# High halves of first-layer weights at their buffers' release, two decodings a phase, and other buffers for phase 8's turned tiles

## Chip, core and metric

The kernel runs on one core of a Trainium2 chip. The metric is the device time of one execution in microseconds (us). The engines are TensorE (PE), VectorE (DVE), ScalarE (ACT), GpSimd (POOL) and SyncE (SP); SP issues all the DMAs of this kernel.

## What is computed

An attention with decaying state, then a layer of eight experts with normalized weights P, then a last layer with a two-sided activation. Everything is float32. This is the reference, cut to what matters here:

```python
x = attention(q, k, v)                        # 1536 x 512
for e in range(8):                            # moe_w1: 512 x 1024, moe_w2: 1024 x 512 each
    h = np.maximum(x @ w1[e], 0.0)
    out += P[:, e:e + 1] * (h @ w2[e])
h = out @ w_in                                # 512 x 2048
g = np.maximum(h, 0.0) + alpha * np.minimum(h, 0.0)
return g @ w_out                              # 2048 x 512
```

w_in and w_out come as 64-bit floats; the kernel turns them into 32-bit floats itself. That is the decoding below.

## The kernel before

**Phases.** After the attention, 20 phases follow one another. Phases 0 to 7 are the eight experts on the first 768 tokens, 8 to 15 the eight experts on the other 768, 16 and 17 the two halves of the last layer on the first tokens, 18 and 19 the same on the others. Phases 8 to 15 are called fast (`FAST`): they also use seven products instead of eight in the second layer. The others are called slow.

**Split numbers.** Each float32 matrix is split into a high part (ACT copies it to the matmul's reduced format) and a low part (the rest, a subtraction on DVE or POOL). `mm3` (line 195) multiplies high x high, high x low and low x high, so each pair of matrices costs three matmuls.

**Product stage.** Every phase begins with it. The first layer is done with seven products instead of eight (a scheme of sums and differences of quarter matrices), for four column groups j = 0 to 3, n = 4 x phase + j. So there are 28 products (j, p) with p = 1 to 7. Each is six matmuls of 384 columns. The order is written out by hand in `order` (line 902). A place in it is called a position here:

```
0 (0,1)   1 (0,5)   2 (0,6)   3 (0,2)   4 (0,7)   5 (1,1)   6 (1,5)
7 (0,4)   8 (1,6)   9 (0,3)  10 (1,2)  11 (1,7)  12 (2,1)  13 (2,5)
14 (1,4) 15 (2,6)  16 (1,3)  17 (2,2)  18 (2,7)  19 (3,1)  20 (3,5)
21 (2,4) 22 (3,6)  23 (2,3)  24 (3,2)  25 (3,7)  26 (3,3)  27 (3,4)
```

`after` (line 686) is what follows each product. After p = 1, ACT copies bank A to a new bank B (line 698), and p = 6, 7 and 4 add to B. After p = 5, ACT copies bank D to `d` (line 693 in the fast phases and those of experts). After p = 6, DVE makes bank E = B + d (line 701). Product (j,7) may then add to B. After p = 7, DVE makes D = B + d (line 714, slow) or `b22` = B + d (line 709, fast), and (j,4) may then add to B. After p = 2, 3, 4 ACT takes the result out.

**Second half.** In a slow phase it is layer 2: six blocks t of tokens, each in two half-blocks `t0a`, `t0`, ... `t5`, of 12 matmuls of 512 columns each. DVE adds each block's result to `total` (line 749). Positions 28 to 39 are these half-blocks. In a fast phase it is `fast2` (line 829), 28 units of six matmuls of 384 columns, on seven pieces `hs` of the hidden layer that ACT (`hhigh`) and DVE (`t1` to `t4`, `hlow`) make of `b11`, `b12`, `b21`, `b22`. Positions 28 to 55 are these units. Its results, weighted by DVE (line 823), are added to `total` by POOL in the next phase (`gather`, line 825). A position of 60 or more is a position of the next phase (60 is 0).

**What is hung in.** `step(ph, pos, fn)` (line 911) hangs a piece of work behind a position; within one position the pieces come in the order in which they were registered. Every engine runs its own instructions strictly in this order (`tc.manual_schedule`), and waits for the semaphores of the data and the buffers that it needs. The pieces are:
- `w1_at` (line 937): for one n, the sums of first-layer weights (`w1_adds`, not in the fast phases, which read them ready), then high and low halves of the parts a (A11, A12, used by p = 1, 2), c (W1 to W3, used by p = 5, 6, 7) and b (A22, W4, used by p = 4, 3). The tiles `wa`, `wb`, `wc` have two buffers a tag (`wp`), so the tile for n + 2 takes the buffer of n. The low half of part b also asks for the raw tile of n + 2 (`w_load`).
- the second layer's weights: `w2_high`, `w2_low`, `w2_keep` (stored for the fast phases).
- `prep_at` (line 926): for one piece of the second layer's weights, the sums for the fast phases (two and two, on DVE or POOL), the load of the next piece, the high half (ACT), two low halves (DVE) and the store. There are 32 pieces, five a phase in phases 1 to 6, two in phase 7.
- `decode_at` (line 918): one of 32 units of w_in and w_out. `bits` is three DVE operations, `power` one of ACT, `join` two of DVE, `store` a store of 256 KB and the load of the next unit (512 KB, tile `rd`, one buffer). The unit's tiles `ex` and `a` have the tag `tmp`, which has two buffers.
- `turn` (line 884): at the end of phase 7 and the start of phase 8 it turns `total` (three transpositions on PE, a copy on ACT into a tile with the tag `tmp`, a store), eight times.

The order around the change is this part of the loop over phases:

```python
            if fast:
                w1_at(ph, n + 2, pool, dve, 0, 2, 3, 3, 5, 5, 7)
                w1_at(ph, n + 3, pool, dve, 5, 9, 14, 10, 15, 12, 16)
...
                decode_at(ph, *((11, 13, 14, 16) if ph == E else (9, 11, 12, 13)))
                decode_at(ph, *((22, 24, 26, 27) if ph == E else (20, 22, 23, 25)))
                if ph < 2 * E - 1:
                    decode_at(ph, 53, 55, 60, 61)
```

The numbers of `w1_at` are the positions of the sums, then of high and low for a, c and b. Those of `decode_at` are bits, power, join and store.

Of the kernel before, what the change touches and what calls it, by code (L numbers as in the profile page):

```python
# [8 lines left out]
F32 = mybir.dt.float32  # L9
# [35 lines left out]
def tile_kernel(ctx, tc, qkT, kv, ctab, w_gate, w1, w2, w_in, w_out, alpha, out):  # L45
# [246 lines left out]
    with tc.manual_schedule():  # L292
# [591 lines left out]
        def turn(g, a, h):  # L884
            ps = bank(f"tr{g}_{a}{h}")
            for q in range(3):
                nc.tensor.matmul(
                    ps[:, 128 * q:128 * q + 128], acc[3 * h + q][:, 128 * a:128 * a + 128], ident,
                    start=(q == 0), stop=(q == 2), is_transpose=True, skip_group_check=True,
                )  # L890
            t = tp.tile([128, HT], F32, tag="tmp", name=f"tt{g}_{a}{h}")
            nc.scalar.activation(out=t, in_=ps[:, 0:HT], func=AF.Copy)
            nc.sync.dma_start(out=xd[g][:, a, HT * h:HT * h + HT], in_=t)

# [23 lines left out]
        def decode_at(ph, *at_):  # L918
            if todo:
                u = todo.pop(0)  # L920
                for pos, fn in zip(at_, decode_steps(u, todo[0] if todo else None)):
                    step(ph, pos, fn)
# [21 lines left out]
        for ph in range(len(PHASES)):  # L944
            n = NJ * ph
            fast = ph in FAST
            eng = dve if fast else pool
            if ph == 0:
                decode_at(ph, 9, 11, 13, 14)
                decode_at(ph, 21, 23, 25, 26)  # L950
            elif ph < E:
                decode_at(ph, *((32, 34, 36, 37) if ph < 7 else (15, 17, 19, 21)))
                prep_at(ph, dve, 9, 14, 9, 17, 20, 21, 26)
                prep_at(ph, pool, 25, 25, 25, 29, 30, 30, 31)
                if ph < 7:
                    prep_at(ph, dve, 31, 31, 31, 33, 34, 34, 35)
                    prep_at(ph, dve, 35, 35, 34, 37, 38, 38, 39)
                    prep_at(ph, pool, 37, 37, 37, 39, 61, 61, 63)
            if fast:
                w1_at(ph, n + 2, pool, dve, 0, 2, 3, 3, 5, 5, 7)  # L960
                w1_at(ph, n + 3, pool, dve, 5, 9, 14, 10, 15, 12, 16)
                w1_at(ph, n + 4, pool, dve, 36, 36, 38, 39, 40, 42, 43)
                w1_at(ph, n + 5, pool, dve, 44, 44, 45, 48, 49, 50, 52)
            else:
                w1_at(ph, n + 2, pool, pool, 0, 3, 3, 6, 6, 9, 9)
                w1_at(ph, n + 3, pool, pool, 5, 10, 10, 12, 12, 16, 16)
                if ph > 0:
                    w1_at(ph, n + 4, dve, dve, 29, 29, 30, 31, 32, 31, 32)
                    w1_at(ph, n + 5, dve, dve, 33, 33, 34, 35, 36, 35, 36)
                early = ((4, 6, 7, dve), (9, 12, 13, dve), (15, 16, 19, dve), (22, 23, 24, dve))  # L970
                usual = ((12, 12, 12, pool), (17, 17, 17, pool), (19, 19, 19, pool), (23, 23, 23, pool))
                for j, (hi, l0, l1, eng) in enumerate(early if 0 < ph < E else usual):
                    step(ph, hi, lambda m=n + j: w2_high(m))
                    step(ph, l0, lambda m=n + j, eng=eng: w2_low(m, 0, eng))
                    step(ph, l1, lambda m=n + j, eng=eng: w2_low(m, 1, eng))
                if ph < E:
                    for j, pos in enumerate((19, 22, 29, 31)):
                        step(ph, pos, lambda m=n + j: w2_keep(m))
            if fast:
                decode_at(ph, *((11, 13, 14, 16) if ph == E else (9, 11, 12, 13)))  # L980
                decode_at(ph, *((22, 24, 26, 27) if ph == E else (20, 22, 23, 25)))
                if ph < 2 * E - 1:
                    decode_at(ph, 53, 55, 60, 61)
                if ph > E + 1:
                    for q in range(8):
                        step(ph, (1, 4, 6, 8)[q // 2], lambda m=q // 2, h=q % 2: gather(m, h))
                step(ph, 0, lambda ph=ph: weight_load(ph))
                for pos, fn, jp in ((17, t1, 0), (21, t2, 0), (25, t3, 0), (27, t1, 1), (30, t2, 1), (31, t3, 1)):
                    step(ph, pos, lambda ph=ph, fn=fn, jp=jp: fn(ph, jp))
                highs = (11, 25, 19, 28, 22, 31, 32, 34, 36, 38, 41, 43, 47, 49)  # L990
                lows = (13, 26, 20, 29, 24, 32, 33, 35, 37, 39, 42, 44, 48, 50)
                for k in range(14):
                    step(ph, highs[k], lambda ph=ph, k=k: hhigh(ph, k))
                    step(ph, lows[k], lambda ph=ph, k=k: hlow(ph, k))
                for pos, jp in ((34, 0), (36, 1)):
                    step(ph, pos, lambda ph=ph, jp=jp: t4(ph, jp))
                if ph in (E + 1, E + 4):
                    step(ph, 0, lambda k=(ph - E - 1) // 3: xk.extend(x_keep(2, k)))
                if E < ph < 2 * E - 1:
                    for keys in ((12, 17, 18, 27), (37, 39, 41, 45), (46, 48, 50, 55)):  # L1000
                        i = unit[0] - NJ * E
                        if i >= 7 * ((ph - E - 1) // 3 + 1):
                            continue
                        unit[0] += 1
                        for q, pos in enumerate(keys):
                            step(ph, pos, lambda i=i, q=q: xk[i][q]())
            if ph + 1 in XGROUP:
                g = XGROUP[ph + 1]
                if g == 2:
                    at(ph, 0, lambda: new_x(2))  # L1010
                    for i, u in enumerate((1, 4, 7, 10, 13, 15, 16, 18, 19, 21, 22, 24, 25, 27)):
                        q = (B11, T1, T2, B21, T3, T4, B22)[i // 2]
                        at(ph, u, lambda q=q, w=i % 2: x_fetch(2, q, w))
                    continue
                bb = {}
                at(ph, (3, 7), lambda g=g, bb=bb: bb.update({0: x_load(g, 0)}))
                at(ph, "t0", lambda g=g, bb=bb: (new_x(g), x_sums(g, 0, *bb[0]), bb.update({1: x_load(g, 1)})))
                at(ph, "t2", lambda g=g, bb=bb: x_sums(g, 1, *bb[1]))
# [2 lines left out]
        at(0, "t5", lambda: prep_load(0))  # L1021
        for w in range(6):
            at(E, ((0, 7), (1, 5), (1, 6), (1, 2), (2, 1), (2, 6))[w], lambda w=w: ws_load(E, w))
        for a, (key, later) in enumerate(zip(("t3", "t4", "t4", "t5"), (order[i] for i in (0, 1, 5, 6)))):
            at(E - 1, key, lambda a=a: turn(2, a, 0))
            at(E, later, lambda a=a: turn(2, a, 1))
        at(1, (0, 2), spread_copy)
# [121 lines left out]
```

## Time and profile before

| | us |
|---|---|
| median of 3 runs | 1340.89 (1340.35 to 1342.67) |
| the profiled execution | 1340.84 |
| its span, first to last instruction | 1338.9 |

| engine | busy us | share of the span | instructions |
|---|---|---|---|
| PE | 1293.1 | 97% | 7179 |
| DVE | 973.0 | 73% | 1552 |
| ACT | 634.0 | 47% | 1129 |
| POOL | 444.1 | 33% | 393 |

The mean granted clock of PE is 0.994 of 2.4 GHz; DMA moves 222 GB/s over the span. A busy share is an average over stages that differ. Idle time of an engine that isn't the bound costs nothing; where PE is busy nearly all the time, its rare waits are what can be won, and each has its place in the order above.

### The profile page before, as it was taken

What the parts mean: (1) busy time and instruction counts of PE and PEld (TensorE: products, weight loads), DVE (VectorE), ACT (ScalarE), POOL (GpSimd) and SP (SyncE); (2) the same over time, 40 slices, a digit from 0 to 9 for tenths busy, and PEclk for the clock granted to TensorE, in tenths of its full rate; (3) what the DMA queues carried; (4) which work ended last, traced back from release to release, by engine and by line L of the source; (5) the groups of instructions that cost most, each with busy time, mean ns of one, the idle gap of its engine ahead of it and who ended that gap; (6) DMA issues with size and microseconds to landing.
All of it is one profiled execution on the core that took longest, in us unless ns stands there. A gap on an engine that the chain in (4) does not pass through costs nothing.

```text
span 1338.9 us, 19554 instructions
## 1 busy us (share of the span) xinstructions
PE 1293.1 (97%) x7179; PEld 1191.4 (89%) x7179; DVE 973.0 (73%) x1552; ACT 634.0 (47%) x1129; POOL 444.1 (33%) x393
## 2 busy tenths in 40 slices
PE   9889999999999999999999999999999999999998
PEld 6788989898988889789998989899999998989897
DVE  5657767777777777838697979797888975586361
ACT  2452626253544444446464554545464554556370
POOL 4860525253342526000023222240403373425160
PEclk9999999999999999999999999999999999999999
DMA  9464698989898888856867768685857573143211
GB/s 361 172 210 150 193 303 271 317 269 318 261 310 269 297 285 289 268 184 231 280 208 266 227 227 274 206 293 185 304 176 265 186 279 95 61 137 102 62 32 47
DMA packets 152255, 296.80 MB, mean 222 GB/s; under 512 B 11952, under 2 KB 77024, under 8 KB 152160
## 3 DMA queue, kind: packets, MB, share of 16 engines
q1 hardware_dynamic: 152160, 295.57, 66.6%
q8 instruction: 56, 0.92, 0.3%
q14 instruction: 39, 0.32, 0.1%
HBM read 198.24 MB, written 97.28 MB: 221 GB/s over the span
## 4 chain that ended last, share of the span: by engine, by line
PE 75%; DVE 10%; DMA 4%; POOL 4%; issue 3%; ACT 3%; SPq 0%; DVEq 0%; POOLq 0%; ACTq 0%
PE o L196 10%; PE o L198 10%; PE o L197 10%; PE B L196 7%; PE B L198 6%; PE B L197 6%; PE A L196 4%; PE A L198 4%; PE A L197 4%; PE D L197 2%; PE D L198 2%; PE D L196 2%; PE E L197 2%; PE E L196 2%; PE E L198 2%
## 5 line engine op out<-in xcount | busy, mean ns | idle before, releaser
L106 POOL TENSOR_TENSOR raw<-raw 128x256 f32<-128x256 f32 x108 | 91.7, 859 | 96.6 <-DMA raw<-wd 42.9
L178 POOL TENSOR_TENSOR pr<-pr 128x256 f32<-128x256 f32 x52 | 51.6, 992 | 197.8 <-DMA pr<-in_w_dram 162.6
L827 POOL TENSOR_TENSOR total<-total,t 128x384 f32<-128x384 f32 x56 | 75.6, 1375 | 113.0 <-DVE t L823 112.9
L785 ACT ACTIVATE hs<-b 128x768 fp32r<-128x768 f32 x112 | 93.8, 845 | 36.5 <-PE A L198 11.4
L795 DVE TENSOR_TENSOR hs<-b,hs 128x768 fp32r<-128x768 f32 x96 | 93.4, 980 | 13.8 <-ACT hs L785 13.7
L749 DVE SCALAR_TENSOR_TENSOR total<-o,P,total 128x512 f32<-128x512 f32 x42 | 31.5, 749 | 70.4 <-PE o L198 69.7
L260 POOL TENSOR_TENSOR xs<-b,xs 128x384 fp32r<-128x384 f32 x6 | 7.9, 1311 | 207.9 <-ACT xs L256 207.9
L701 DVE TENSOR_TENSOR E<-B,d 128x384 f32<-128x384 f32 x80 | 45.0, 563 | 42.4 <-PE B L198 26.9
L182 ACT ACTIVATE pw<-pr 128x1024 fp32r<-128x1024 f32 x32 | 33.8, 1057 | 88.2 <-issue 51.2
L698 ACT ACTIVATE B<-A 128x384 f32<-128x384 f32 x80 | 38.6, 483 | 58.3 <-PE A L198 56.5
L198 PE MATMUL B<-hs,ws 128*128 128x384 f32 x192 | 64.2, 335 | 0.0
L196 PE MATMUL B<-hs,ws 128*128 128x384 f32 x192 | 64.2, 334 | 0.0
L197 PE MATMUL B<-hs,ws 128*128 128x384 f32 x192 | 64.2, 334 | 0.0
L604 ACT ACTIVATE ex<-ex,ebias 128x512 uint32<-128x512 uint32 x32 | 22.9, 715 | 60.0 <-DVE ex L594 60.0
L186 DVE TENSOR_TENSOR pr<-pr,pw 128x512 fp32r<-128x512 f32 x64 | 49.6, 815 | 0.0
L178 DVE TENSOR_TENSOR pr<-pr 128x256 f32<-128x256 f32 x76 | 45.5, 598 | 1.7
L743 ACT ACTIVATE total<-o 128x512 f32<-128x512 f32 x18 | 10.8, 598 | 68.8 <-PE o L198 68.8
L714 DVE TENSOR_TENSOR D<-B,d 128x384 f32<-128x384 f32 x48 | 26.9, 560 | 22.5 <-PE B L198 22.5
L196 PE MATMUL A<-hs,ws 128*128 128x384 f32 x128 | 42.9, 335 | 0.0
L197 PE MATMUL A<-hs,ws 128*128 128x384 f32 x128 | 42.9, 335 | 0.0
L198 PE MATMUL A<-hs,ws 128*128 128x384 f32 x128 | 42.9, 335 | 0.0
L106 DVE TENSOR_TENSOR raw<-raw 128x256 f32<-128x256 f32 x84 | 36.9, 457 | 1.4
(3435 smaller groups left out, 4711.9 us busy)
## 6 DMA issues: line engine op xcount, KB each, us to landing
ws<-c SPq DMA_DIRECT2D x112, 512.0 KB, 5.0
raw<-in_w_dram SPq DMA_DIRECT2D x64, 512.0 KB, 4.3
c<-raw SPq DMA_DIRECT2D x32, 512.0 KB, 5.6
pr<-in_w_dram SPq DMA_DIRECT2D x32, 512.0 KB, 6.1
c<-pw SPq DMA_DIRECT2D x32, 512.0 KB, 7.4
c<-pr SPq DMA_DIRECT2D x32, 512.0 KB, 7.4
raw<-c SPq DMA_DIRECT2D x32, 512.0 KB, 5.7
raw<-wd SPq DMA_DIRECT2D x32, 512.0 KB, 3.7
```

Source lines behind the costliest of these rows:

```text
L106: eng.tensor_tensor(out=out, in0=in0, in1=in1, op=op)
L178: eng.tensor_tensor(out=out, in0=in0, in1=in1, op=op)
L182: nc.scalar.activation(out=ph2[i], in_=pr[i], func=AF.Copy)
L186: nc.vector.tensor_tensor(out=pr[i][:, a].bitcast(F32R), in0=pr[i][:, a], in1=ph2[i][:, a].bitcast(F32), op=ALU.subtract)
L196: nc.tensor.matmul(ps, ah, bh, start=first, stop=False, skip_group_check=True)
L197: nc.tensor.matmul(ps, ah, bl, start=False, stop=False, skip_group_check=True)
L198: nc.tensor.matmul(ps, alo, bh, start=False, stop=last, skip_group_check=True)
L698: nc.scalar.activation(out=banks[n, "B"], in_=banks[n, "A"], func=AF.Copy)
L701: nc.vector.tensor_tensor(out=banks[n, "E"], in0=banks[n, "B"], in1=banks[n, "d"], op=add)
L785: nc.scalar.activation(out=t[:, 0, :], in_=hsource(ph, k), func=func)
L795: nc.vector.tensor_tensor(out=lo, in0=src, in1=hi.bitcast(F32), op=ALU.subtract)
L827: nc.gpsimd.tensor_tensor(out=dst, in0=dst, in1=tt[m, h], op=ALU.add)
```

## The change

- In the fast phases the high halves of n + 2 go from 2, 3, 5 (parts a, c, b) to 3, 4, 9, the low ones from 3, 5, 7 to 4, 6, 10. For n + 3 the high ones go from 9, 10, 12 to 10, 11, 16, the low ones from 14, 15, 16 to 12, 13, 17.
- The 32 decodings are dealt out anew: one in phase 0 (two before), two in the second half of phases 1 to 6 (one before), one in the second half of phase 7 (one in its product stage before), two in each of phases 8 to 15 (three before, two in phase 15), two in the second half of phase 16.
- The first preparation of phases 1 to 7 makes its second pair of sums at 19 instead of 14, and what follows it moves back too, as do two low halves of second-layer weights.
- The turned tiles with a = 2, 3 take buffers of the tag `pu`, which the loads of x use, and the later ones go at positions 3 and 4 of phase 8 instead of 5 and 6.
- The gathers go from positions 1, 4, 6, 8 to 2, 5, 8, 11.

```diff
@@ turn
-            t = tp.tile([128, HT], F32, tag="tmp", name=f"tt{g}_{a}{h}")
+            if a < 2:
+                t = tp.tile([128, HT], F32, tag="tmp", name=f"tt{g}_{a}{h}")
+            else:
+                t = tp.tile([128, S], F32, tag="pu", bufs=2, name=f"tt{g}_{a}{h}")[:, 0:HT]
@@ loop over the phases
             if ph == 0:
                 decode_at(ph, 9, 11, 13, 14)
-                decode_at(ph, 21, 23, 25, 26)
             elif ph < E:
-                decode_at(ph, *((32, 34, 36, 37) if ph < 7 else (15, 17, 19, 21)))
-                prep_at(ph, dve, 9, 14, 9, 17, 20, 21, 26)
+                if ph < 7:
+                    decode_at(ph, 30, 31, 32, 33)
+                decode_at(ph, 36, 37, 38, 39)
+                prep_at(ph, dve, 9, 19, 9, 21, 23, 24, 27)
...
+            elif ph == 2 * E:
+                decode_at(ph, 30, 31, 32, 33)
+                decode_at(ph, 36, 37, 38, 39)
             if fast:
-                w1_at(ph, n + 2, pool, dve, 0, 2, 3, 3, 5, 5, 7)
-                w1_at(ph, n + 3, pool, dve, 5, 9, 14, 10, 15, 12, 16)
+                w1_at(ph, n + 2, pool, dve, 0, 3, 4, 4, 6, 9, 10)
+                w1_at(ph, n + 3, pool, dve, 5, 10, 12, 11, 13, 16, 17)
...
-                early = ((4, 6, 7, dve), (9, 12, 13, dve), (15, 16, 19, dve), (22, 23, 24, dve))
+                early = ((4, 6, 7, dve), (9, 12, 13, dve), (15, 16, 20, dve), (22, 25, 26, dve))
...
             if fast:
-                decode_at(ph, *((11, 13, 14, 16) if ph == E else (9, 11, 12, 13)))
-                decode_at(ph, *((22, 24, 26, 27) if ph == E else (20, 22, 23, 25)))
-                if ph < 2 * E - 1:
-                    decode_at(ph, 53, 55, 60, 61)
+                decode_at(ph, 5, 7, 8, 10)
+                decode_at(ph, 19, 21, 23, 25)
                 if ph > E + 1:
                     for q in range(8):
-                        step(ph, (1, 4, 6, 8)[q // 2], lambda m=q // 2, h=q % 2: gather(m, h))
+                        step(ph, (2, 5, 8, 11)[q // 2], lambda m=q // 2, h=q % 2: gather(m, h))
@@ behind the loop
-        for a, (key, later) in enumerate(zip(("t3", "t4", "t4", "t5"), (order[i] for i in (0, 1, 5, 6)))):
+        for a, (key, later) in enumerate(zip(("t3", "t4", "t4", "t5"), (order[i] for i in (0, 1, 3, 4)))):
```

## Rows read from the trace of the kernel before

**Rows 1.** Waits of PE in total: who <- releaser: us, times, longest.

```profile
PE B L196 <- DVE E L701: 28.3, 31, 4.4
```

**Rows 2.** By stage: start:end length, busy (instructions) per engine, PEclk, DMA share, GB/s.

```profile
618.36:647.51 29.15, 29.15 (x169) 29.15 (x169) 26.59 (x38) 14.62 (x22) 0.00 (x0) 1.00 0.82 276
...
63.87:101.85 37.98, 33.41 (x175) 32.00 (x175) 20.62 (x39) 19.22 (x35) 24.63 (x22) 0.91 0.70 222
...
sum 181.72, PE 177.46 PEld 174.84 DVE 155.14 ACT 116.59 POOL 107.46; mean PE 29.58 PEld 29.14 DVE 25.86 ACT 19.43 POOL 17.91
...
514.75:547.98 33.23, 30.35 (x170) 29.07 (x169) 29.24 (x45) 19.27 (x35) 17.97 (x16) 1.00 0.86 283
...
708.61:742.22 33.61, 30.54 (x170) 28.95 (x170) 26.02 (x37) 17.39 (x33) 8.90 (x7) 1.00 0.63 216
...
sum 267.88, PE 246.21 PEld 234.84 DVE 197.15 ACT 138.41 POOL 58.26; mean PE 30.78 PEld 29.36 DVE 24.64 ACT 17.30 POOL 7.28
```

**Rows 3.** Timeline of PE, phase 10: start, us, what, count [idle before <-releaser].

```profile
714.33 0.45 PE L196 MATMUL B<-xh,wc40h 128*128 128x384 f32 x1 [1.37 <-DVE E L701]
...
722.66 0.45 PE L196 MATMUL B<-xh,wc41h 128*128 128x384 f32 x1 [0.77 <-DVE E L701]
...
730.70 0.45 PE L196 MATMUL B<-xh,wc42h 128*128 128x384 f32 x1 [0.48 <-DVE E L701]
...
734.32 0.44 PE L196 MATMUL B<-xh,wb42h 128*128 128x384 f32 x1 [0.23 <-DVE b L709]
```

**Rows 4.** Timeline of ACT, phase 10, in front of the stall at 722.66.

```profile
720.77 0.63 ACT L126 ACTIVATE wb42h<-raw 128x512 fp32r<-128x512 f32 x1 [3.57 <-PE E L197]
721.30 0.47 ACT L693 ACTIVATE d<-D 128x384 f32<-128x384 f32 x1
```

**Rows 5.** Timeline of POOL and DVE, start of phase 10: gathers and a decoding's last operation.

```profile
710.82 5.25 POOL L827 TENSOR_TENSOR total<-total,t 128x384 f32<-128x384 f32 x4 [1.56 <-DVE t L823]
...
712.42 1.38 DVE L613 SCALAR_TENSOR_TENSOR a<-rd,a 128x512 uint32<-128x512 uint32 x1
```

**Rows 6.** Instructions on the tile rd: ns min/median/max, first and last start; landing.

```profile
L613 DVE SCALAR_TENSOR_TENSOR a<-rd,a x32: 691/693/1391, 81.4 to 1049.6; 128x512 uint32<-128x512 uint32 x32
...
DMA to landing us min/median/max: 3.8/5.3/9.0
```

**Rows 7.** Phase 0: timelines of PE, DVE and ACT, and a window at the fallen clock.

```profile
96.17 0.69 PE L196 MATMUL B<-xh,wc3h 128*128 128x384 f32 x1 [4.37 <-DVE E L701]
...
93.97 0.62 DVE L594 TENSOR_SCALAR ex<-rd 128x512 uint32<-128x512 uint32 x1 [6.68 <-DMA rd<-in_w_in_dram]
...
90.68 1.06 ACT L145 ACTIVATE v2h<-raw 128x1024 fp32r<-128x1024 f32 x1 [3.57 <-DMA raw<-in_w_dram]
...
98.00:100.00 2.00, 2.00 (x8) 2.00 (x7) 1.50 (x3) 0.49 (x1) 2.00 (x2) 0.50 1.09 382
```

**Rows 8.** Phase 2: timelines of PE, DVE and POOL around the stall at (2,7).

```profile
219.76 0.44 PE L196 MATMUL B<-xh,wc10h 128*128 128x384 f32 x1 [0.66 <-DVE E L701]
...
218.36 0.87 DVE L178 TENSOR_TENSOR pr<-pr 128x256 f32<-128x256 f32 x2
...
220.42 3.99 POOL L178 TENSOR_TENSOR pr<-pr 128x256 f32<-128x256 f32 x4
```

**Rows 9.** Phase 2's layer 2 as a window, then POOL, ACT, DVE into phase 3.

```profile
230.29:262.94 32.65, 32.65 (x145) 27.06 (x145) 22.25 (x40) 9.01 (x12) 6.07 (x7) 1.00 0.93 300
...
256.56 4.51 POOL L178 TENSOR_TENSOR pr<-pr 128x256 f32<-128x256 f32 x4 [32.15 <-DMA pr<-in_w_dram]
...
261.10 1.06 ACT L182 ACTIVATE pw<-pr 128x1024 fp32r<-128x1024 f32 x1 [5.23 <-POOL pr L178]
...
264.18 0.47 ACT L698 ACTIVATE B<-A 128x384 f32<-128x384 f32 x1 [2.02 <-PE A L198]
...
266.33 0.57 DVE L701 TENSOR_TENSOR E<-B,d 128x384 f32<-128x384 f32 x1 [1.08 <-PE B L198]
```

## What I expect, before the run

> **What bounds the kernel.** TensorE does. I read the profile in three steps. First the page: PE is busy 97% of the span, so only its idle time can be won. Then the waits of PE added up: one entry holds most of its idle time, products that wait for DVE's sum E at line 701 [rows 1]. Last the busy time by stage, with the boundaries set where the first matmul of each stage starts [rows 2]. This is the view that the sum rests on. The second half of a fast phase is 168 matmuls of 384 columns, and it takes 29.15 us with nothing lost. A product stage is also 168 matmuls of 384 columns, so whatever it takes above 29.15 us is loss. Phase 0's takes 37.98 (8.83 lost), those of phases 1 to 6 together 181.72 (6.82 lost), phase 7's 33.23 (4.08 lost), those of the eight fast phases together 267.88 (34.68 lost) [rows 2]. That is 54.4 us. Layer 2 and the second halves lose next to nothing.
>
> The idle time that a row shows is less than what a stall costs, since the ends of matmuls are modelled. Phase 10's stage takes 33.61 us, 4.46 lost [rows 2], in five stalls; four show 1.37 + 0.77 + 0.48 + 0.23 us [rows 3] and the fifth, at (3,4), is like the fourth, together 3.08. So each costs some 0.28 more than its row says.
>
> **Why it stalls.** Product (j,7) adds to bank B, which DVE must have read first for E, and DVE needs d, ACT's copy of D. So (j,7) waits for the chain ACT d, DVE E. In phase 10, ACT was idle for 3.57 us in front of the high half wb42h until a product on E ended, and copied d right behind it [rows 4]. That product is (0,3), the last reader of the part-b weights of j = 0, whose buffer wb42h takes (two buffers a tag): the high half is issued at position 5, its buffer comes free at position 9, and d of (1,5), position 6, is queued behind. The same holds for j = 3 (issued at 12, free at 16). These are the stalls 0.77 and 0.48 at (1,7) and (2,7) [rows 3].
>
> **Part 1, the high halves in the fast phases.** They now stand at 3, 4, 9 and 10, 11, 16, each at the last product that reads the buffer. ACT no longer waits with d behind it. Then d of (1,5) is done about 0.5 us (one such copy [rows 4]) after that product ends, and E at position 8 comes straight behind (1,6). What is late next: the low halves move back by 1 to 4 positions on DVE, wb of j = 2 to 10 (first needed at (2,4), 21), wb of j = 3 to 17 (needed at 26). The next raw tile is asked for in the same step; its first reader is at 36. Both have cover of 8 us or more. If it were gone, the price would be a stall of the size seen, 0.5 to 1 us. The part of the loss removed is (0.77 + 0.48 + 2 x 0.28) x 8 = 14.5 us.
>
> **Part 2, the third decoding leaves the fast phases.** A decoding is five DVE operations of at most 0.69 us [rows 6], under 3.5 us, one ACT operation, a load and a store. The third one's last two operations came at position 0, in front of E of (0,6). While POOL gathered (four in 5.25 us), one of them took 1.38 us [rows 5] against a median of 0.69 [rows 6]. That makes the 1.37 us at (0,7) [rows 3]. With them gone nothing that long stands in front of E. The remaining decodings, at 5 to 10 and 19 to 25, have the same operations in nearly the same order as before.
>
> What stays is DVE's own queue from 17 to 27. Low half wb, t1, b22, three operations of the decoding, a low half of hidden, t2, E, two of the decoding, a low half and b22 follow one another without a break. They make the small stalls at (2,4) and (3,4), 0.23 each [rows 3], about 1.0 us a phase with the 0.28. The chain starts some 0.4 us earlier, since it no longer waits for a late E. Bounds are 0 and 1.0; nothing makes it much shorter, so I take 0.7. Phase 8 has four turned tiles in its product stage: each is one 384-column matmul's worth, 0.17 us, to twice that; I take 1.4 for the four. The eight stages then lose 1.4 + 8 x 0.7 = 7.0 instead of 34.7: **gain 27.7**. The buffers for the turned tiles belong here. They let the last four go at positions 0, 1, 3, 4 and free the decoding's two buffers by position 5. The PE work is the same, so they have no term of their own.
>
> Moving the gathers from 1, 4, 6, 8 to 2, 5, 8, 11 costs and gains nothing: POOL has nothing else to do there, and it runs each one when its data is there, wherever it stands in the order.
>
> **Part 3, phase 0.** The second decoding's first operation waited 6.68 us for its load, with E behind it, and PE waited 4.37 [rows 7]. Then the granted clock was 0.50, the 1.2 GHz level [rows 7]. The 18 matmuls from 96.17 to the stage's end at 101.85 took 5.68 us instead of 18 x 29.15/168 = 3.12. So the stall cost 4.37 + 0.28 + 2.56 = 7.2. Late next: ACT's high half v2h, which waited for its DMA and started at 90.68 [rows 7], with d behind it. With 1.0 for v2h, 0.5 for d [rows 4] and 0.6 for E [rows 9], E ends near 92.7; PE was ready at 96.17 - 4.37 = 91.8. That is a stall of 0.9 + 0.28. **Gain 6.0.**
>
> **Part 4, phases 1 to 7.** In phase 2, two sums of the preparation (0.87 us) ran just before E, and (2,7) waited 0.66 [rows 8]. They move from 14 to 19, behind that E. There they meet POOL's sums (four in 3.99 us, [rows 8]), which start about then whatever their position. Alone they cost 0.87, stretched perhaps 2.5; E of (3,6) has 1.5 us of room, so I take no stall. The low halves that move to 23 to 26 displace each other one for one. Phase 7 also loses the decoding from its product stage (15 to 21). The turned tiles' copies in its layer 2 may wait for the decoding's buffers, on an ACT that is otherwise idle.
>
> **Part 5, the second decoding in layer 2 of phases 1 to 6.** DVE is busy 22.25 of 32.65 us there, so 3.5 us more fit. DMA is not so free: its share is 0.93 at 300 GB/s [rows 9]. A load of 512 KB and a store of 256 KB add 2.6 us to its queue, in front of the load for POOL's last sums. Those started at 256.56, when that load landed; ACT's copy of them ended at 262.16; ACT's B came at 264.18, and the first E at 266.33 after 1.08 us of idle time [rows 9]. So ACT has 2.0 us of room and needs 2.6, then DVE's low halves and E follow. That is 0 to 1.5 us at the start of a phase; I take 0.5, nearer to the room that the row shows. The decoding's own load has three half-blocks, 3 x 32.65/12 = 8.2 us, from issue to use; loads took 5.3 in the median and 9.0 at most [rows 6]. Phases 1 to 6 lose 6.82 now, then 0.3 for a transposition in phase 1 and 5 x 0.5: **gain 4.0**. Phase 7: 4.08 to 0.5, **gain 3.6**.
>
> **Part 6, phase 16.** Two decodings in its layer 2, where DVE has little to do: nothing.
>
> **Sum.** 27.7 + 6.0 + 4.0 + 3.6 = 41.3 us. The profiled execution took 1340.84 (span 1338.9 and 1.9 around it), within 0.1 of the median, so no correction. 1340.8 - 41.3 = 1299.5: **1300 us**. If every stall went, 51 would be gained, 1290.
>
> **Rivals.**
> *DVE's queue becomes the bound of the fast phases.* For it: in the stage just behind, DVE is busy 26.59 of 29.15 us [rows 2], and the chain from 17 to 27 has no gap. Against it: the change takes some 3 us a phase away. A phase would lose 2.0 instead of 0.7: 8 x 1.3 more, 1310.
> *The change doesn't free ACT*, because another wait takes the buffer's place (d late for another reason). Against it: the wait's releaser [rows 4] is exactly the buffer's last reader. The 14.5 us stay: 1314.
> *Gathers meet the decodings.* Six phases gather; if the gathers run beside positions 5 to 8, the decoding's operations last 1.38 instead of 0.69 [rows 5, 6], E of (1,6) comes up to 3.4 us later than with none, of which about 1 us is past its room: 6 x 1.0, 1306. Against it: the gathers wait for data that is there at the phase's start, and should be through by position 6. The Trainium skill (SBUF — State Buffer, "Who interferes with whom") says that of a VectorE and a GpSimd instruction that want the shared ports, the one that comes second is blocked until the first has finished. By that rule a decoding so placed pays up to a whole gather (5.25/4 = 1.3 us) per operation; the trace's 1.38 against 0.69 is a little over half of that.
> *Slower.* In layer 2 of phases 1 to 6 the second load lands so late that DVE, standing at its first operation, holds up the copies, the low halves and the next phase's first E by over 4 us, and the clock falls as in phase 0. Each costs phase 0's 7.2 us: 6 x 7.2 = 43 against 41 gained, 1343. It decides from a landing of 8.2 + 2 + 4 = 14 us; the longest seen is 9.0 [rows 6], but the queue is fuller.
>
> **How the numbers follow.** Forecast 0.58 (1291 to 1305), DVE's queue 0.17, gathers 0.12, ACT not freed 0.07, the slower case 0.06 (of which 0.01 ends within 0.2% of no change). The range goes from 1291 (all stalls gone but a few) to 1320, past the first three rivals, with room for two together. Faster by over 0.2% (2.7 us, about what a measurement of this kernel can tell): 0.94; within it 0.01; slower 0.05.
>
> **What would show it.** Right: product stages of phases 9 to 15 of 29.5 to 30.5 us; no idle time of ACT before wb in front of d; phase 0's stage near 32 at full clock; phases 1 to 7 with at most a small stall at (0,6) or (0,7). Wrong: stalls at (3,7) or (3,4) of over 1 us (DVE's queue), at (1,7) of phases 10 to 15 only (gathers), or DVE waiting for rd in layer 2 of phases 1 to 6 with a stall at the next (0,7).

## The result, and the profile of the changed kernel

| | us |
|---|---|
| before, median of 4 runs | 1341.28 (1340.35 to 1342.67) |
| after, median of 4 runs | 1298.95 (1298.71 to 1300.12) |
| ratio | 0.9685 [0.9669, 0.9702] |
| the profiled execution after | 1299.14, its span 1297.4 |

The change takes 42.3 us away, 41.5 by the two profiled spans. The page after shows where: PE has the same 7179 matmuls and 13 us less busy time, and it is now busy 99% of the span.

```profile
PE 1280.1 (99%) x7179; PEld 1187.3 (92%) x7179; DVE 961.1 (74%) x1552; ACT 634.6 (49%) x1129; POOL 436.0 (34%) x393
```

The waits of PE added up, after: of the entry of [rows 1], 28.3 us in 31 waits, 0.9 us is left, in one wait. Beside it stands the wait for the sum `b` (line 709).

```profile
PE B L196 <- DVE b L709: 2.3, 5, 1.1
...
PE B L196 <- DVE E L701: 0.9, 1, 0.9
```

The busy time by stage, after, with the columns of [rows 2]: phase 0's product stage and its layer 2, the sum of phases 1 to 6, phase 7's, then phases 8, 10, 11 and 15 and the sum of the eight fast ones.

```profile
63.59:95.69 32.10, 31.02 (x175) 29.60 (x176) 16.32 (x31) 16.09 (x30) 22.17 (x20) 1.00 0.64 200
95.69:131.68 35.99, 35.54 (x164) 28.85 (x164) 25.93 (x93) 9.49 (x17) 5.45 (x6) 1.00 0.49 168
...
sum 177.84, PE 177.64 PEld 174.61 DVE 155.21 ACT 118.81 POOL 119.31; mean PE 29.61 PEld 29.10 DVE 25.87 ACT 19.80 POOL 19.89
...
505.50:535.04 29.54, 29.54 (x169) 29.07 (x168) 26.30 (x39) 19.04 (x35) 20.16 (x18) 1.00 0.90 305
569.03:599.62 30.59, 30.59 (x183) 30.45 (x182) 20.46 (x32) 19.06 (x36) 0.00 (x0) 1.00 0.78 269
...
687.72:717.51 29.79, 29.50 (x169) 29.09 (x169) 21.25 (x32) 17.26 (x32) 6.98 (x7) 1.00 0.64 217
746.66:775.84 29.18, 29.18 (x170) 29.18 (x170) 20.62 (x32) 17.39 (x32) 5.82 (x6) 1.00 0.62 219
...
981.19:1011.75 30.56, 29.45 (x169) 29.13 (x169) 21.99 (x32) 16.86 (x31) 10.98 (x12) 1.00 0.47 157
...
sum 238.70, PE 236.44 PEld 234.32 DVE 168.65 ACT 139.74 POOL 45.62; mean PE 29.55 PEld 29.29 DVE 21.08 ACT 17.47 POOL 5.70
```

Loss is again what a product stage takes above 29.15 us (6 x 29.15 and 8 x 29.15 for the sums):

| product stages | lost before | lost after | gain | gain forecast |
|---|---|---|---|---|
| phase 0 | 8.83 | 2.95 | 5.9 | 6.0 |
| phases 1 to 6 | 6.82 | 2.94 | 3.9 | 4.0 |
| phase 7 | 4.08 | 0.39 | 3.7 | 3.6 |
| phases 8 to 15 | 34.68 | 5.50 | 29.2 | 27.7 |
| sum | 54.4 | 11.8 | 42.6 | 41.3 |

Phase 0's layer 2 takes 35.99 us where it took 35.26 before, so 0.7 of the gain is given back there. Small differences elsewhere make up the other 0.4 to the 41.5 of the spans. This is its row of the kernel before:

```profile
101.85:137.11 35.26, 35.26 (x164) 28.95 (x163) 24.97 (x91) 7.40 (x13) 3.00 (x4) 1.00 0.40 136
```

The timelines show why. ACT in phase 10: the high half wb42h runs without idle time in front of it, where it had kept ACT idle for 3.57 us [rows 4], and `d` is copied 3.5 us before it. Between the two, DVE's E of (1,6) waits for PE alone (the third row), and PE doesn't stall.

```profile
695.23 0.49 ACT L693 ACTIVATE d<-D 128x384 f32<-128x384 f32 x1 [0.56 <-PE D L198]
...
698.74 0.63 ACT L126 ACTIVATE wb42h<-raw 128x512 fp32r<-128x512 f32 x1
...
697.38 0.57 DVE L701 TENSOR_TENSOR E<-B,d 128x384 f32<-128x384 f32 x1 [0.81 <-PE B L198]
```

Phase 0, ACT and PE: v2h still waits for its DMA, `d` stands behind it, and PE waits 0.89 us for E, where it waited 4.37 [rows 7]. The granted clock of the stage is 1.00, not 0.91. The last row is new: layer 2's first product of `mx` waits.

```profile
90.34 1.06 ACT L145 ACTIVATE v2h<-raw 128x1024 fp32r<-128x1024 f32 x1 [3.49 <-DMA raw<-in_w_dram]
...
92.43 0.44 PE L196 MATMUL B<-xh,wc3h 128*128 128x384 f32 x1 [0.89 <-DVE E L701]
...
99.03 0.49 PE L541 MATMUL mx<-dm,ones 128*128 128x128 f32 x2 [0.45 <-DVE mx L529]
```

### The profile page after: what moved, and what is told of

The parts are those of the page before. It is cut to its first block, busy times and chain, and to the rows that moved or that the text cites. A ratio compares the mean times of both kernels' runs of the same rounds, so it can differ in the third digit from the quotient of the medians.

```text
span 1297.4 us, 19511 instructions
## 1 busy us (share of the span) xinstructions
PE 1280.1 (99%) x7179; PEld 1187.3 (92%) x7179; DVE 961.1 (74%) x1552; ACT 634.6 (49%) x1129; POOL 436.0 (34%) x393
## 4 chain that ended last, share of the span: by engine, by line
PE 83%; DVE 5%; POOL 4%; ACT 3%; DMA 2%; issue 2%; SPq 0%; POOLq 0%; DVEq 0%; ACTq 0%
PE o L196 10%; PE o L198 10%; PE o L197 10%; PE B L196 8%; PE B L198 7%; PE B L197 7%; PE A L196 5%; PE A L198 5%; PE A L197 5%; PE D L198 3%; PE D L197 3%; PE D L196 3%; PE E L198 2%; PE E L197 2%; PE E L196 2%
## 5 line engine op out<-in xcount | busy, mean ns | idle before, releaser
L106 POOL TENSOR_TENSOR raw<-raw 128x256 f32<-128x256 f32 x108 | 96.2, 901 | 95.5 <-issue 33.3
L827 POOL TENSOR_TENSOR total<-total,t 128x384 f32<-128x384 f32 x56 | 66.3, 1210 | 103.0 <-DVE t L823 102.9
L186 DVE TENSOR_TENSOR pr<-pr,pw 128x512 fp32r<-128x512 f32 x64 | 52.9, 858 | 0.0
L693 ACT ACTIVATE d<-D 128x384 f32<-128x384 f32 x64 | 31.2, 488 | 15.9 <-PE D L198 15.9
```

What stands on the lines that cost most here:

```text
L106: eng.tensor_tensor(out=out, in0=in0, in1=in1, op=op)
L186: nc.vector.tensor_tensor(out=pr[i][:, a].bitcast(F32R), in0=pr[i][:, a], in1=ph2[i][:, a].bitcast(F32), op=ALU.subtract)
L827: nc.gpsimd.tensor_tensor(out=dst, in0=dst, in1=tt[m, h], op=ALU.add)
```

## The experiments

Each starts from the kernel before ("before +") or from the changed one ("after +"). Losses are those of product stages, worked out as above.

### Before + the new places of the high and low halves alone

```diff
-                w1_at(ph, n + 2, pool, dve, 0, 2, 3, 3, 5, 5, 7)
-                w1_at(ph, n + 3, pool, dve, 5, 9, 14, 10, 15, 12, 16)
+                w1_at(ph, n + 2, pool, dve, 0, 3, 4, 4, 6, 9, 10)
+                w1_at(ph, n + 3, pool, dve, 5, 10, 12, 11, 13, 16, 17)
```

> The kernel before with the new positions of the first-layer high and low halves in the fast phases and nothing else. Theory: ACT was held by the buffer of part b with d queued behind it, so the stalls at (1,7) and (2,7) go in all eight fast phases: (0.77 + 0.48 + 2 x 0.28) x 8 = 14.5 us less than before, 1326 to 1327; the stalls at (0,7) and those of phases 0 to 7 stay. Rival, DVE's own queue is the bound of these stages: the stalls come back at (2,4), (3,7) or (3,4) and at most half is gained, 1334. Rival, something else holds d: no gain, 1341.

Measured: 1320.69 us (1320.38 to 1321.07), ratio 0.9846 [0.9831, 0.9860], 20.3 us less than the kernel before beside it (1340.98). The eight fast stages by sum, and what is left of the five stalls of phase 10 [rows 3]; there are only these two:

```profile
sum 247.98, PE 238.73 PEld 233.92 DVE 193.68 ACT 141.61 POOL 53.94; mean PE 29.84 PEld 29.24 DVE 24.21 ACT 17.70 POOL 6.74
...
706.68 0.44 PE L196 MATMUL B<-xh,wc40h 128*128 128x384 f32 x1 [1.38 <-DVE E L701]
...
731.23 0.44 PE L196 MATMUL B<-xh,wb43h 128*128 128x384 f32 x1 [0.30 <-DVE b L709]
```

The stalls at (1,7) and (2,7) are gone, as forecast, and so is the small one at (2,4), which I had put down to DVE's queue. The stall at (0,7) is untouched. The fast stages gain 267.88 - 247.98 = 19.9 us where 14.5 were forecast. Phase 8 holds most of the difference: its loss falls from 7.29 to 1.72. These are its rows of the kernel before, two on ACT, one on DVE, one on PE, and a window of 2 us behind the stall:

```profile
602.27 0.63 ACT L126 ACTIVATE wb35h<-raw 128x512 fp32r<-128x512 f32 x1 [3.15 <-PE E L197]
602.81 0.47 ACT L693 ACTIVATE d<-D 128x384 f32<-128x384 f32 x1
...
603.92 0.69 DVE L610 SCALAR_TENSOR_TENSOR a<-a,ex 128x512 f32<-128x512 f32 x1 [1.18 <-ACT ex L604]
...
605.87 0.45 PE L196 MATMUL B<-xh,wc34h 128*128 128x384 f32 x1 [2.42 <-DVE E L701]
...
608.00:610.00 2.00, 2.00 (x8) 2.00 (x7) 0.61 (x2) 0.54 (x2) 0.00 (x0) 0.50 0.81 194
```

There too a high half kept `d` waiting, but that is not the whole of this stall. `d` was ready at 603.28, and E began only at 605.25, straight behind two operations of the decoding on DVE. The first of them (603.92) had waited for ACT's `ex`, which stood on ACT behind the same high half and `d`. So it took both, the held ACT and the decoding in front of E. The stall of 2.42 us also brought the clock down to 0.50, which makes it the dearest of the eight stages. I had looked at phase 10 alone for the size of this term, and left phase 8's long stall to the decoding.

### Before + part b's high and low halves alone

```diff
-                w1_at(ph, n + 2, pool, dve, 0, 2, 3, 3, 5, 5, 7)
-                w1_at(ph, n + 3, pool, dve, 5, 9, 14, 10, 15, 12, 16)
+                w1_at(ph, n + 2, pool, dve, 0, 2, 3, 3, 5, 9, 10)
+                w1_at(ph, n + 3, pool, dve, 5, 9, 14, 10, 15, 16, 17)
```

> The kernel before with only part b moved: its high halves from 5 and 12 to 9 and 16, its low halves from 7 and 16 to 10 and 17; parts a and c stay where they were. Theory: of the three parts only b is issued long before its buffer's last reader (4 positions early, a and c one), so it alone gives nearly the whole 14.5 us, 1326 to 1329. Rival, each of the three early high halves holds ACT: a third to a half of it, 1334 to 1336.

Measured: 1320.98 us (1319.66 to 1322.36), ratio 0.9848 [0.9833, 0.9862]. That is the whole gain of the run above, again more than was forecast. The moves of parts a and c do nothing that can be measured; part b's two high halves a phase, which waited for a buffer, and the two low halves made from them do it all.

The low halves matter too, which the forecast had not seen. In phase 10 of the kernel before, the first of them stood on DVE in front of E of (1,6):

```profile
721.43 0.69 DVE L135 TENSOR_TENSOR wb42l<-raw,wb42h 128x512 fp32r<-128x512 f32 x1 [4.04 <-ACT wb42h L126]
```

`d` was ready at 721.77 [rows 4], but E began at 722.04, straight behind this low half. At (2,7) the low half comes behind E, and E waits for `d` alone. That 0.27 us is about the difference between the two stalls, 0.77 and 0.48 [rows 3]. No run moves the high halves without the low ones; by the order of the kernel, a low half left at position 7 would still have held E at 8.

### Before + phase 0's second decoding moved to phase 16

```diff
                 decode_at(ph, 9, 11, 13, 14)
-                decode_at(ph, 21, 23, 25, 26)
...
+            elif ph == 2 * E:
+                decode_at(ph, 30, 31, 32, 33)
```

> The kernel before with one decoding in phase 0 instead of two; the last of the 32 then runs in layer 2 of phase 16. Theory: the stall of 4.37 us at (3,7) shrinks to about 0.9, and the half clock behind it goes with it (2.56 us): 6.0 us less than before, 1335, and a granted clock of 1.00 all through phase 0. Rival, the clock falls for another reason than this stall: 3.5 us less, 1337.6, with windows at 0.50 still there.

Measured: 1336.29 us (1334.62 to 1337.80), ratio 0.9964 [0.9951, 0.9977], 4.7 us less. Phase 0's product stage and its layer 2, then PE's wait in layer 2:

```profile
62.67:94.90 32.23, 30.98 (x175) 29.57 (x176) 16.30 (x31) 16.07 (x30) 22.12 (x20) 1.00 0.60 199
94.90:131.17 36.27, 35.62 (x164) 28.84 (x163) 26.07 (x93) 9.49 (x17) 5.44 (x6) 1.00 0.51 167
...
98.41 0.49 PE L541 MATMUL mx<-dm,ones 128*128 128x128 f32 x2 [0.61 <-DVE mx L529]
```

The stage gains 37.98 - 32.23 = 5.75 of the 6.0 forecast, and the stall left in it is 1.05 us, by v2h with `d` behind it, as forecast. But layer 2 loses 36.27 - 35.26 = 1.0 of it again. `mx` is cleared by DVE behind the low halves of the hidden layer, which wait for ACT; and ACT has v3h in front, which waits for its DMA (3.30 us in the changed kernel, start 95.83). Before, the long stall in front had hidden this chain. The forecast stopped one step too early.

### Before + the decodings alone

```diff
-                decode_at(ph, *((11, 13, 14, 16) if ph == E else (9, 11, 12, 13)))
-                decode_at(ph, *((22, 24, 26, 27) if ph == E else (20, 22, 23, 25)))
-                if ph < 2 * E - 1:
-                    decode_at(ph, 53, 55, 60, 61)
+                decode_at(ph, 5, 7, 8, 10)
+                decode_at(ph, 19, 21, 23, 25)
```

with the other phases' `decode_at` lines and the turned tiles' buffers as in the change; the high halves, the preparation and the gathers stay as before.

> The kernel before with the decodings dealt out anew and the turned tiles' buffers and places, nothing else. Theory: phase 0 gains 6.0; phases 10 to 15 lose their stall at (0,7), four of 1.37 and two of 0.65 with 0.28 each, 8.5; phase 8 loses its long stall at (2,7), 2.42 with its half clock, about 4; phase 7 loses 2 to 3 that its decoding made: about 21 us less than before, 1320. The stalls at (1,7), (2,7) of the fast phases and at (2,7) of phases 1 to 6 stay. Rival, the second decoding in layer 2 of phases 1 to 6 costs at each next phase's start: 0.5 to 1.5 us in six phases, 1323 to 1329.

Measured: 1320.82 us (1320.06 to 1322.17), ratio 0.9850 [0.9833, 0.9866], 20.2 us less. The fast stages and phase 10's stalls:

```profile
sum 255.85, PE 242.63 PEld 233.48 DVE 169.25 ACT 135.24 POOL 47.73; mean PE 30.33 PEld 29.18 DVE 21.16 ACT 16.90 POOL 5.97
...
708.15 0.44 PE L196 MATMUL B<-xh,wc41h 128*128 128x384 f32 x1 [0.77 <-DVE E L701]
...
716.18 0.44 PE L196 MATMUL B<-xh,wc42h 128*128 128x384 f32 x1 [0.48 <-DVE E L701]
...
719.81 0.44 PE L196 MATMUL B<-xh,wb42h 128*128 128x384 f32 x1 [0.21 <-DVE b L709]
...
726.55 0.44 PE L196 MATMUL B<-xh,wb43h 128*128 128x384 f32 x1 [0.23 <-DVE b L709]
```

This is the mirror of the first run: the stall at (0,7) is gone, and the other four stay with the sizes of [rows 3]. The two parts act on different stalls, so they add up, save in phase 8, whose long stall needed both causes, so that either one takes most of the loss: 5.6 (high halves) and 4.1 (decodings) alone, 5.9 together. With the preparation (3.9, below) 20.3 + 20.2 + 3.9 - 3.8 = 40.6 us, against 42.3 measured; the 1.7 between them is of the size of the runs' spread.

### After, and after + the gathers at their old positions

```diff
-                        step(ph, (2, 5, 8, 11)[q // 2], lambda m=q // 2, h=q % 2: gather(m, h))
+                        step(ph, (1, 4, 6, 8)[q // 2], lambda m=q // 2, h=q % 2: gather(m, h))
```

> The changed kernel once more, unaltered, as the measure for the others of this call: 1298 to 1300.

> The changed kernel with the gathers back at positions 1, 4, 6, 8. Theory: POOL runs a gather when its data is there, wherever it stands among DVE's and PE's work, so nothing changes: 1299, and gathers and decoding lie as they did. Rival, gathers are paced by their position and now meet the decoding at 5 to 8: about 1 us at (1,7) in six phases, 1305.

Measured side by side: the changed kernel 1299.62 us (1298.24 to 1299.69), with the gathers moved back 1300.66 (1298.96 to 1301.60), ratios 0.9684 [0.9669, 0.9698] and 0.9692 [0.9678, 0.9707]. The losses of the fast stages agree within 0.2 us. The gathers' position in the order is indeed no matter: POOL runs each when its data is there. In phase 10 of the changed kernel, the last six gathers end at 692.07, 2 us before the decoding's first operation:

```profile
685.76 6.31 POOL L827 TENSOR_TENSOR total<-total,t 128x384 f32<-128x384 f32 x6
...
694.22 0.42 DVE L594 TENSOR_SCALAR ex<-rd 128x512 uint32<-128x512 uint32 x1
```

### After + the old preparation of phases 1 to 7

```diff
-                prep_at(ph, dve, 9, 19, 9, 21, 23, 24, 27)
+                prep_at(ph, dve, 9, 14, 9, 17, 20, 21, 26)
...
-                early = ((4, 6, 7, dve), (9, 12, 13, dve), (15, 16, 20, dve), (22, 25, 26, dve))
+                early = ((4, 6, 7, dve), (9, 12, 13, dve), (15, 16, 19, dve), (22, 23, 24, dve))
```

> The changed kernel with the first preparation and the two low halves of second-layer weights of phases 1 to 7 back where they were. Theory: the two sums (0.87 us) stand in front of E of (2,6) again, and (2,7) waits 0.66 + 0.28 in each of seven phases, against 0.1 to 0.2 lost there now: about 5 us more, 1304. Rival, the stall came from the decodings or from a late d, and stays away: 1299.

Measured: 1303.48 us (1302.55 to 1304.52), ratio 0.9715 [0.9701, 0.9730], 3.9 more than the changed kernel beside it. The stall of [rows 8] is back in phase 2, with the same size, and one like it in each of the phases 1 to 7:

```profile
213.77 0.44 PE L196 MATMUL B<-xh,wc10h 128*128 128x384 f32 x1 [0.65 <-DVE E L701]
```

### After + the second load of phases 1 to 6 with less cover

In the changed kernel the second decoding of these phases begins at 36, three half-blocks behind the place in the order where its load is asked for. Two kernels take cover away, one half-block (35) and two (34):

```diff
-                decode_at(ph, 36, 37, 38, 39)
+                if ph < 7:
+                    decode_at(ph, 35, 36, 37, 38)
+                else:
+                    decode_at(ph, 36, 37, 38, 39)
```

and the same with 34, 35, 36, 37. The text for 35 was written behind the one for 34 and refers to it.

> The same with 35 to 38, half as tight: DVE comes to the load near 246.6 and stands 2.4 us; only the two pairs of sums (1.8 us) move behind the landing. Theory: E of (0,6) is about 1.2 us late, 6 x (1.2 + 0.28) = 9 us more, 1308. Rival, slack in layer 2 takes it: 1299 to 1300.

> The changed kernel with the second decoding of phases 1 to 6 at 34 to 37 instead of 36 to 39, so that its first operation comes one half-block behind the load instead of three. This is the slower rival's mechanism, made to happen. The load still lands about 249.0 in the changed kernel's phase 2, and DVE comes to it near 242.8. Theory: DVE stands 6.2 us, and 4.5 us of its queue (low halves, a copy, sums) that was done before the load landed now comes after it; its room up to the next phase's E is about 0.6 us, so E of (0,6) is about 3.9 us late, (0,7) waits as long in six phases: 6 x (3.9 + 0.28) = 25 us more, 1324, and up to 2.5 more in each phase if the clock falls, 1339. Rival, DVE has slack in layer 2 and no one waits for it there: 1299 to 1302.

Measured: with 35, 1317.45 us (1315.69 to 1319.21), ratio to before 0.9827 [0.9809, 0.9844]; with 34, 1341.69 us (1338.02 to 1344.69), ratio 1.0004 [0.9994, 1.0015]. Two half-blocks of cover are worth the whole change. First with 35: DVE's wait for `rd` in the layer 2 of phase 1, PE's stall in phase 3, and a window of 2 us behind that stall. Then with 34: the wait in phase 1, and a window behind the stall that follows in phase 2.

```profile
186.78 0.43 DVE L594 TENSOR_SCALAR ex<-rd 128x512 uint32<-128x512 uint32 x1 [2.40 <-DMA rd<-in_w_in_dram]
...
266.19 0.44 PE L196 MATMUL B<-xh,wc12h 128*128 128x384 f32 x1 [1.83 <-DVE E L701]
268.00:270.00 2.00, 2.00 (x8) 2.00 (x7) 1.51 (x4) 1.59 (x3) 1.74 (x3) 0.50 1.09 386
```

```profile
186.77 0.43 DVE L594 TENSOR_SCALAR ex<-rd 128x512 uint32<-128x512 uint32 x1 [6.22 <-DMA rd<-in_w_in_dram]
...
204.00:206.00 2.00, 2.00 (x8) 2.00 (x8) 0.45 (x1) 0.00 (x0) 1.85 (x3) 0.50 0.99 325
```

The six phases of the three kernels, DVE's wait for `rd` and the stall of PE at the next (0,7), in us:

| kernel | waits for rd | stalls |
|---|---|---|
| after (36) | 0.73, 0.61, 0.98, 0.65, 1.66, 0.61 | none |
| 35 | 2.40, 2.23, 2.60, 2.52, 3.83, 2.46 | 2.08, 1.83, 2.28, 1.30, 4.59, 2.11 |
| 34 | 6.22, 6.54, 6.87, 6.13, 7.34, 6.36 | 4.58, 5.34, 5.35, 4.62, 5.34, 5.33 |

Behind waits of up to 1.66 us no stall follows; from 2.2 on half of the wait or more comes back as a stall, and in one phase more than the wait (4.59 behind 3.83). With 34 each stage loses 7.1 to 9.3 us, 2.2 to 3.9 more than the stall in the table, most of it at the clock of 0.50. My expectations were too low in both parts: the stalls that I put at 1.2 and 3.9 us measured 1.30 to 4.59 and 4.58 to 5.35, and the clock cost more. The price in the prediction itself, 7.2 us each, was the right one.

### After + the last stalls aimed at

The stalls left in the fast phases stand at (3,4), behind the second decoding's last two operations. This kernel moves them behind that product, and in phase 0 it moves v2h (the high half of j = 2) behind the `d` that E needs:

```diff
+                j2 = 22 if ph == 0 else 19
-                usual = ((12, 12, 12, pool), (17, 17, 17, pool), (19, 19, 19, pool), (23, 23, 23, pool))
+                usual = ((12, 12, 12, pool), (17, 17, 17, pool), (j2, j2, j2, pool), (23, 23, 23, pool))
...
-                decode_at(ph, 19, 21, 23, 25)
+                decode_at(ph, 19, 21, 27, 28)
```

> The changed kernel with two more moves: in the fast phases the second decoding's join and store go from 23, 25 to 27, 28, behind b22 of (3,7), and in phase 0 the high half v2h goes from 19 to 22, behind d of (3,5). Theory: the stall at (3,4), 0.29 in four fast phases and 1.11 in phase 15, each with 0.28, goes or shrinks (2 to 3.5 us), and phase 0's stall at (3,7), 0.89 + 0.28, goes: 1294.5 to 1296. Rival, DVE's queue only hands the wait on, to the first units of the second half or to (3,7): 1298 to 1299.

Measured: 1296.28 us (1295.34 to 1297.83), ratio 0.9663 [0.9647, 0.9679], 3.3 less than the changed kernel beside it. The fast stages' sum, phase 0's two stages and the wait in the second of them:

```profile
sum 234.95, PE 234.95 PEld 234.44 DVE 159.30 ACT 139.72 POOL 46.10; mean PE 29.37 PEld 29.30 DVE 19.91 ACT 17.47 POOL 5.76
...
63.05:93.91 30.86, 30.66 (x175) 29.59 (x175) 16.40 (x31) 16.31 (x30) 22.14 (x20) 1.00 0.65 209
93.91:131.25 37.34, 35.52 (x164) 28.82 (x164) 25.92 (x93) 9.50 (x17) 5.40 (x6) 1.00 0.50 162
...
98.62 0.49 PE L541 MATMUL mx<-dm,ones 128*128 128x128 f32 x2 [1.82 <-DVE mx L529]
```

In the fast stages all stalls are gone: PE is busy for the whole 234.95 us, and the 1.75 above 8 x 29.15 are nearly all the turned tiles' work in phase 8. In phase 0 nothing is won: the stage takes 1.2 less, layer 2 takes 1.4 more, by the same wait for `mx`. A last kernel also clears `mx` earlier, in front of those low halves:

```diff
-        at(0, (3, 4), lambda: sums.update(ps=zeroed("mx", 128)))
+        at(0, (3, 2), lambda: sums.update(ps=zeroed("mx", 128)))
```

> The version with join and store of the second decoding at 27, 28 and v2h at 22 in phase 0, and one more move: the clearing of the bank mx goes from behind (3,4) to behind (3,2) of phase 0, so that it stands on DVE ahead of the low half that waits for v3h's load. Theory: the wait of PE for mx, 1.82 us where v2h moved, goes; 1.9 to 2.1 us less than the 1296.3 without this move, 1294.3. Rival, the wait moves to the matmul's other input, to layer 2's low halves, or to a missing bank: 1296.

Measured: 1295.23 us (1294.14 to 1295.73), ratio 0.9658 [0.9645, 0.9671]: faster than both kernels. The step from the one above (0.9663) is inside the intervals; layer 2 takes 0.5 us less. The wait for `mx` is gone, but layer 2 now waits at the next place where PE needs a bank that DVE clears:

```profile
94.44:131.25 36.81, 35.54 (x164) 28.83 (x163) 25.65 (x92) 9.48 (x17) 5.50 (x6) 1.00 0.52 165
...
101.63 0.39 PE L563 MATMUL cs<-s,ones 128*128 128x8 f32 x2 [1.27 <-DVE cs L529]
```

## Why the prediction was right, point by point

The forecast was 1300 us with a gain of 41.3; the time is 1298.95 with a gain of 42.3. The mechanisms are in the main the forecast ones. That the sum is right to about 1 us is in part luck, since the fast phases give 1.5 more than forecast while 0.7 is lost again in phase 0's layer 2 and 0.4 elsewhere.

**What bounds the kernel, and the loss of 54.4 us.** Right. The same view after leaves 11.8, and nearly all that is gained is gained in product stages. That a stall costs some 0.28 more than its row holds for a short one too: phase 10's stage after loses 29.79 - 29.15 = 0.64 us with one stall of 0.29, so 0.35 more.

**Part 1, high halves.** The mechanism is right: ACT, held by a buffer, kept `d`. It is not complete: at (1,7) DVE's low half, which waited for the same high half, kept E some 0.3 us longer. The runs with part 1 and with part b alone show the gain. The term was mis-sized: 14.5 forecast, 19.9 measured. 3.8 of the 5.4 between them are phase 8's, whose stall of 2.42 us at the fallen clock came from the held ACT and the decoding together and was not counted here. The rest, 0.2 a phase on average, is mainly the stall at (2,4), which goes as soon as `d` is on time and so belonged to ACT and not to DVE's queue.

**Part 2, the third decoding.** Right for (0,7). Phase 9 of the kernel before bears it out: there the third decoding's last two operations stand in front of E as well, but POOL gathers nothing. They take 0.68 and 0.69 us, E waits 1.33 us for PE, and PE doesn't stall at (0,7). It took the decoding and the gathers together. The decodings alone give 267.88 - 255.85 = 12.0 us in the fast stages. The 27.7 was worked out from what stays (34.7 - 7.0) and not from the parts, so the wrong size of part 1 did not enter it, and it came out at 29.2.

**What stays in the fast phases.** 7.0 forecast, 5.5 measured. The turned tiles' 1.4 is 30.59 - 29.15 = 1.44, with 14 matmuls more than phase 10 and no idle time. DVE's unbroken chain does make a stall at (3,4), and moving two of its operations takes it away (1296.28). But it costs 0.64 in four phases, next to nothing in phases 11 and 14, and 1.41 in phase 15, instead of 0.7 in each. In phases 10 and 11 DVE runs the same 32 operations in 21.25 and 20.62 us. Phases 9, 10, 12 and 13, which have the stall, have two POOL operations beside the chain, `xs` (1.47 us) and `ta` or `tb` (1.20 us); phases 11 and 14, which have none, have `xs` alone. The DVE operation that meets the second one (L596) takes 1.24 us in the four and 0.41 to 0.42 in the two. So the difference is how much of POOL's work falls on the chain. I argue this from these rows and from the stretched operations below; no run takes POOL's operations away.

**Gathers.** Right: no cost and no gain.

**Part 3, phase 0.** Right to 0.1 us for the stage (E late by 0.89 behind v2h, 0.9 forecast). What failed is "late next": the list ended with the stage, and 0.7 us are lost again in layer 2, mostly at `mx`.

**Part 4.** Right: 3.9 us by taking it back.

**Part 5, the second decoding in layer 2.** The gain of phases 1 to 6 is right (3.9 for 4.0), by a different make-up. The 0.5 us charged to each phase's start is not there; in its place the stages of phases 2 to 6 lose 0.4 each, with no idle time in a row, and phase 1's 0.9. DVE after, the first E of phase 3:

```profile
260.03 0.57 DVE L701 TENSOR_TENSOR E<-B,d 128x384 f32<-128x384 f32 x1 [0.23 <-PE B L198]
```

DVE does wait for `rd` in the layer 2 in front, 0.61 us (table above), and the first E still comes with 0.23 us to spare, where [rows 9] had 1.08. In this phase the room was used up almost to the end, not overrun. That DVE waits at all shows a step that failed: the load's cover was not the 8.2 us that part 5 counted, as the next point shows.

**The slower rival.** It did not come, but the runs with 35 and 34 made its mechanism happen, and its price holds: with 34 the loss is 1341.69 - 1299.62 = 42.1 us, 7.0 a phase, the whole gain. Its condition, a landing of 14 us, does not hold, since it took the load to be issued when its place in the order comes. In phase 2's layer 2 after, the half-block at position 33 ends at 240.32. SP issues its DMAs in order and comes to this load at 242.68, and DVE is at its first operation 0.61 us before 249.04, so at 248.43:

```profile
242.68 0.43 SPq L584 DMA_DIRECT2D rd<-in_w_in_dram  x1
...
249.04 0.43 DVE L594 TENSOR_SCALAR ex<-rd 128x512 uint32<-128x512 uint32 x1 [0.61 <-DMA rd<-in_w_in_dram]
```

That is a cover of 5.75 us instead of 8.2. Over the six phases it is 5.1 to 5.9 us after, 3.2 to 4.1 with 35 and next to nothing with 34, while from issue to that operation it takes 6.2 to 7.0 us in all three kernels. So an ordinary load already makes DVE wait, and only DVE's slack keeps it from costing. An estimate from the table, where stalls begin between waits of 1.66 and 2.2: a landing 0.5 to 1.6 us longer would have begun to cost. The forecast saw 5 us between the longest landing of 9.0 and its edge of 14; there was far less, so this rival was nearer than its chance of 0.06 says.

**The other rivals.** DVE's queue and ACT fell with the losses above; one sign of DVE's queue, a stall at (3,4) of over 1 us, did appear, in phase 15 alone (1.11). The gathers could not meet the decoding, since they are through 2 us earlier (phase 10, above).

## What to carry to other kernels

An instruction that waits for a buffer holds everything behind it on its engine, and what waits for its result holds the next engine: put both at the last reader of that buffer, and look there first when a short copy on a half-idle engine is late. Count a term over all the stages that it touches, not over the typical one; here the one odd stage (phase 8) held over a quarter of it. When a stall is taken away, follow the lateness past the stage's end to the next wait that it had covered, and find how far the cover of a moved load can shrink before the gain is gone: here 5.4 us of cover decided over 42 us. Count cover from the issue on the DMA queue and not from the place in the order: 8.2 us by the order were 5.1 to 5.9 by the queue.

## What the hardware showed

**The clock falls after stalls shorter than I had seen.** Before, it fell to 0.50 after 4.37 us [rows 7], and after 2.42 us in phase 8. With 35, the window 268 to 270 shows 0.50 after a stall of 1.83 us. In the same kernel it stayed at 1.00 after the stalls of 1.30 and 2.11 (phases 5 and 7):

```profile
397.00:399.00 2.00, 1.67 (x9) 1.68 (x10) 0.57 (x2) 0.07 (x1) 1.85 (x2) 1.00 1.09 386
...
530.00:532.00 2.00, 1.65 (x9) 1.65 (x10) 0.58 (x2) 0.00 (x0) 1.92 (x3) 1.00 1.06 377
```

So the length of one stall does not settle it. A stall of about 2 us can cost little more than its row or nearly twice as much: phase 7's stage loses 2.38 us with the stall of 2.11, phase 3's 3.65 with that of 1.83.

**DVE beside POOL.** POOL and DVE in phase 10 after, in the chain in front of (3,4):

```profile
707.65 1.47 POOL L260 TENSOR_TENSOR xs<-b,xs 128x384 fp32r<-128x384 f32 x1 [15.57 <-ACT xs L256]
709.08 1.20 POOL L252 TENSOR_TENSOR tb<-b,b 128x384 f32<-128x384 f32 x1
...
708.62 0.78 DVE L594 TENSOR_SCALAR ex<-rd 128x512 uint32<-128x512 uint32 x1
709.32 1.24 DVE L596 TENSOR_SCALAR a<-rd 128x512 uint32<-128x512 uint32 x1
...
716.34 0.45 PE L196 MATMUL B<-xh,wb43h 128*128 128x384 f32 x1 [0.29 <-DVE b L709]
```

Both DVE operations take 0.42 us when alone; here they take 0.36 and 0.82 more. Each ends 0.28 us after the POOL operation that was running when it began: 709.40 after 709.12, and 710.56 after 710.28. That agrees with the rule of the Trainium skill (SBUF — State Buffer, "Who interferes with whom") by which the second to want the shared ports is blocked until the first has finished. The prediction took "a little over half of a gather" for the price of a meeting; by these two rows it goes by how much of the other's operation is left when the meeting begins. Not every DVE operation pays it: `b` (L709), which reads a bank, ran from 708.15 under the same POOL operation and took 0.55 us, as it does elsewhere.
